# The last chunk's state product of a gated SSM and GELU mix as seven block products, with its block sums on VectorE

## The chip, the cores and the metric

The kernel runs on one core of a Trainium2 chip. The metric is the device time of one execution in microseconds. Before the change it is 211.94 us, the median of 3 runs (211.27 to 212.22). The engines are named as in the profile: PE (TensorE matmuls), PEld (its weight loads), DVE (VectorE), ACT (ScalarE), POOL (GpSimd) and SP (SyncE, which here only issues DMAs).

## The reference

For x of 2048 x 640 in bf16, a gate g mixes a state space layer a and a dense layer b:

```python
g = sigmoid((x * gate_w).sum(-1, keepdims=True))
h[t] = Lam_bar * h[t-1] + B_bar @ x[t]            # 640 complex states
a = 2.0 * (hseq @ Cmat.T).real + x * Dskip
b = gelu(x @ w1 + b1, approximate=True) @ w2 + b2 # 640 -> 1728 -> 640
out = g * a + (1 - g) * b
```

## The kernel before

Time is cut into 4 chunks of 512 rows (`NCH`, `CH`), each into 4 tiles of 128 rows (`TPC`). For each chunk c there are four stages.

- `ssm(c)` multiplies x by B (PE, line 607), copies the results to `bu` (ACT, line 610) and queues the scan for each of 5 groups of 128 states. One group's scan on DVE is `scan_ops`: two products, a sum, two scans (line 555), two products and the last difference into `hs[c]` (all products and sums come from the helper on line 533). Real and imaginary parts are the two halves of `hs[c]`, 1280 rows in all.
- `ff1(c)` is the first dense layer (PE, line 299) with GELU (ACT, line 308). The result `gel[c]` is laid out as two halves of time (i) by two halves of the hidden rows (k): four blocks a, b, g21, d.
- `fin_b(c)` is the second dense layer as seven block products in place of eight (2 x 2 blocks, in the manner of Strassen and Winograd): `both` does a product for the two tiles of a half on PE (line 702), 14 matmuls of 320 columns. Banks X, Y, Q and Z collect the products. `fork` copies a bank on ACT (line 714), `out_of` writes a bank scaled by 1 - g into `gb` on ACT (line 722), `part_7` writes -(1 - g) Q into `gq` on ACT (line 735), and POOL adds that to `gb` by an accumulating DMA (`plus`, line 650). The sums of left blocks, N3 and N2, and the sums g21 + d and b + N2, are made by a negation on ACT (line 655) and accumulating DMAs (`minus_c`, `minus_d`, and `plus(flat(b), flat(N2[:]))` inside `fin_b`). For chunk 0 `first_sums` does them on DVE (line 685). The sums of w2's blocks (TA, TB, TC) are made once, near the start.
- `fin_a(c)` is the state product, row tile by row tile: for each half of the 640 columns 10 matmuls (5 for the real, 5 for the imaginary part, line 775) add to a bank that `seed` has filled with x * Dskip (ACT, line 641; the product with Dskip is `skip`, DVE, line 635). DVE then writes `ot` = g * bank + `gb` (line 780), and SP stores it. The last tile is cut into 320, 192 and 128 columns, and ACT's queue stores the last piece. `ot` has three buffers.

The order of the work is written by hand. Each engine executes its instructions in the order of the calls. Only the scans are placed by a small model: `later` puts an operation on a list with a cost, `let_out(t)` emits what the model's DVE would have started by the model's time t, and `dve_now` first lets out what is due and then emits its own instruction. `Clock` holds the model's times. `fin_a(c)` begins with `let_out(0, c)`, which emits all that is left of chunk c's scans. SP's and POOL's queues take their DMAs in the order of the calls as well, and each waits in its place. `load_xn` on SP brings a tile of x back for the skip term; `seed(ti)` issues the load of tile ti + 5 into the buffer that it frees (five buffers).

The last part of the program is: `ssm(3)`, `ff1(3)`, `gates(3)`, `fin_b(2)`, `fin_a(2)`, `fin_b(3)`, `fin_a(3)`. So PE does chunk 3's states early, while DVE's scans for them run beside `ff1(3)`, `fin_b(2)`, `fin_a(2)` and a part of `fin_b(3)`.

Of the kernel before, what the change touches and what calls it, by code (L numbers as in the profile page):

```python
# [42 lines left out]
def kernel(  # L43
# [25 lines left out]
    ps = ctx.enter_context(tc.tile_pool(name="ps", bufs=8, space=bass.MemoryType.PSUM))  # L69
    hsp = ctx.enter_context(tc.tile_pool(name="hsp", bufs=2))  # L70
    gelp = ctx.enter_context(tc.tile_pool(name="gelp", bufs=2))
    xnp = ctx.enter_context(tc.tile_pool(name="xnp", bufs=5))
    work = ctx.enter_context(tc.tile_pool(name="work", bufs=2))
    fwork = ctx.enter_context(tc.tile_pool(name="fwork", bufs=4))

# [7 lines left out]
    n1c = F - cut2 + 1  # L83
    xA, xB = (const.tile([P, KD, CH], BF16, name=n) for n in ("xA", "xB"))
    xT = [xA, xB, xB, xA]
    w1a = [const.tile([P, cut1], BF16, name=f"w1a_{kd}") for kd in range(KD)]
    w1b = [const.tile([P, cut2 - cut1], BF16, name=f"w1b_{kd}") for kd in range(KD)]
    w1c_lo = const.tile([P, 3, n1c], BF16, name="w1c_lo")
    w1c_hi = const.tile([P, 2, n1c], BF16, name="w1c_hi")
    w1c = [w1c_lo[:, j, :] for j in range(3)] + [w1c_hi[:, j, :] for j in range(2)]  # L90
    w2_sb = const.tile([P, 2, KF, HD], BF16, name="w2_sb")
# [30 lines left out]
    def load_xn(ti):  # L122
        xn[ti] = xnp.tile([P, D], BF16, name="xn")
        nc.sync.dma_start(out=xn[ti][:], in_=x2d[ti * P:(ti + 1) * P, :])
# [2 lines left out]
        nc.sync.dma_start_transpose(out=xT[c][:], in_=x2d[c * CH:(c + 1) * CH, :])  # L127

    def load_w1a(queue, kd):
        queue.dma_start(out=w1a[kd][:], in_=B_w1[kd * P:(kd + 1) * P, 0:cut1])  # L130

    def rows(queue, dst, v):
        queue.dma_start(out=dst, in_=v.rearrange("(j p) -> j p", p=P))
# [25 lines left out]
    load_w1a(nc.sync, 4)  # L159
    load_w1a(nc.sync, 3)  # L160
    for kd in range(KD):
        nc.sync.dma_start(out=w1b[kd][:], in_=B_w1[kd * P:(kd + 1) * P, cut1:cut2])
    for t, k0, k1 in ((w1c_lo, 0, 3), (w1c_hi, 3, KD)):
        nc.sync.dma_start(out=t[:, :, 0:F - cut2], in_=B_w1[k0 * P:k1 * P, cut2:F].rearrange("(k p) f -> p k f", p=P))
    make_identity(nc, ident[:])
    HC = CH // 8
    tfi = work.tile([P, HC], I32, name="e")
    nc.gpsimd.iota(tfi[:], pattern=[[1, HC]], base=0, channel_multiplier=0)
    rows(nc.gpsimd, prmA[0:KS, :], A_log_dt)
    rows(nc.gpsimd, prmA[KS:2 * KS, :], A_Lambda_im)  # L170
# [39 lines left out]
    def load_skip():  # L210
        nc.sync.dma_start(out=Dbc[:], in_=A_Dskip.rearrange("(o d) -> o d", o=1).to_broadcast([P, D]))
        for a in range(TPC):
            load_x0(nc.sync, a, KA * P, D)
        load_xn(TPC)

    ctx.enter_context(tc.manual_schedule(engines={E.PE, E.DVE, E.Activation, E.SP, E.Pool}))

# [22 lines left out]
    def dve_now(ready, cost, fn):  # L240
        let_out(ready)
        fn()
        ck.dve = max(ck.dve, ready) + cost
# [282 lines left out]
    def scan_ops(c, ks, bu, ready):  # L526
        wide = lambda t: t[:, ks:ks + 1, :].to_broadcast([P, 2, CH])
        signed = c > 0
        sines = TSIN2[:, ks, :, :] if signed else wide(TSIN)
        s = {}  # L530

        def tt(o, a, b, op):
            nc.vector.tensor_tensor(out=o, in0=a, in1=b, op=op)  # L533

        def f1():
            s["mc"] = work.tile([P, 2, CH], BF16, name="wa", bufs=1)
            tt(s["mc"][:], wide(TCOS), bu[:], ALU.mult)

        def f2():
            s["ms"] = work.tile([P, 2, CH], BF16, name="wb", bufs=1)  # L540
            tt(s["ms"][:], sines, bu[:], ALU.mult)

        def f3():
            s["v"] = work.tile([P, 2, CH], BF16, name="v", bufs=1)
            if signed:
                return tt(s["v"][:], s["mc"][:], s["ms"][:, ::-1, :], ALU.add)
            tt(s["v"][:, 0, :], s["mc"][:, 0, :], s["ms"][:, 1, :], ALU.add)
            tt(s["v"][:, 1, :], s["mc"][:, 1, :], s["ms"][:, 0, :], ALU.subtract)

        def f4(ri):  # L550
            if ri == 0:
                settle(1)
                s["g"] = work.tile([P, 2, CH], BF16, name="g")
            init = 0.0 if c == 0 else carry[:, ri, ks:ks + 1]
            nc.vector.tensor_tensor_scan(s["g"][:, ri, :], r_c[:, ks:ks + 1].to_broadcast([P, CH]),  # L555
                                         s["v"][:, ri, :], init, ALU.mult, ALU.add)

        def f5():
            g = s["g"]

            def turn_carry():
                m = work.tile([P, 2], F32, name="e1")
                one = lambda out, i, sc, b: nc.scalar.activation(out=out, in_=g[:, i, CH - 1:CH], func=ACT.Identity,
                                                                 scale=sc[:, ks:ks + 1], bias=b)
                one(m[:, 0:1], 1, nsL, 0.0)
                one(m[:, 1:2], 0, sL, 0.0)
                one(carry[:, 0, ks:ks + 1], 0, cL, m[:, 0:1])
                one(carry[:, 1, ks:ks + 1], 1, cL, m[:, 1:2])
                ck.act += 0.6

            small.append((ck.dve + 2.0, turn_carry))

        def f6():
            s["no"] = work.tile([P, 2, CH], BF16, name="wa", bufs=1)
            tt(s["no"][:], wide(TCOS), s["g"][:], ALU.mult)

        def f7():
            s["ns"] = work.tile([P, 2, CH], BF16, name="wb", bufs=1)
            tt(s["ns"][:], sines, s["g"][:], ALU.mult)

        def f8():
            if signed:
                return tt(hs[c][:].rearrange("p (r k) t -> p r k t", r=2)[:, :, ks, :], s["no"][:], s["ns"][:, ::-1, :], ALU.subtract)
            tt(hs[c][:, ks, :], s["no"][:, 0, :], s["ns"][:, 1, :], ALU.subtract)
            tt(hs[c][:, KS + ks, :], s["ns"][:, 0, :], s["no"][:, 1, :], ALU.add)

        later(ready, 0.68, f1)
        later(0, 0.62, f2)
        later(0, 0.65 if signed else 0.7, f3)
        later(0, 1.27, lambda: f4(0))  # L590
        later(0, 1.21, lambda: f4(1))
        if c < NCH - 1:
            later(0, 0.0, f5)
        later(0, 0.69, f6)
        later(0, 0.62, f7)
        later(0, 0.64 if signed else 0.77, f8, c)

    def ssm(c, at={}):
        hs[c] = hsp.tile([P, 2 * KS, CH], BF16, name="hs")
        for ks in range(KS):  # L600
            if ks in at:
                at[ks]()
# [34 lines left out]
    def seed(ti):  # L637
        seeded[ti] = []
        for d0, d1 in cuts(ti):
            p = bank()  # L640
            nc.scalar.activation(out=p[:, 0:d1 - d0], in_=xn[ti][:, d0:d1], func=ACT.Identity)  # L641
            act(0.45)
            seeded[ti].append(p)
        if ti % TPC < TPC - 2:
            skip(ti + 2)
        if ti + 5 < NT:
            load_xn(ti + 5)

    def plus(dst, src):
        nc.gpsimd.dma_start(out=dst, in_=src, accum_op=ALU.add)  # L650
# [110 lines left out]
    def fin_a(c, at={}):  # L761
        let_out(0, c)
        for a in range(TPC):
            ti = c * TPC + a
            lo = a * P
            ot = fwork.tile([P, D], BF16, name="ot", bufs=3)
            if a < TPC - 2:
                seed(ti + 2)
            if a in at:
# [1 line left out]
            for i, (d0, d1) in enumerate(cuts(ti)):  # L771
                p = seeded[ti][i]
                for j in range(2 * KS):
                    CT = CT_re if j < KS else CT_im
                    nc.tensor.matmul(p[:, 0:d1 - d0], lhsT=hs[c][:, j, lo:lo + P], rhs=CT[:, j % KS, d0:d1],  # L775
                                     start=False, stop=(j == 2 * KS - 1), skip_group_check=True)
                    pe(d1 - d0)

# [10 lines left out]
            if ti < NT - 1:  # L789
                nc.sync.dma_start(out=out2d[ti * P:(ti + 1) * P, :], in_=ot[:])  # L790

    def skips(c):
        skip(c * TPC)
        skip(c * TPC + 1)

    def seeds(c, more=lambda: None):
        return {1: lambda: seed(c * TPC), 2: lambda: (seed(c * TPC + 1), more())}
# [23 lines left out]
    fin_a(1, sums(2))  # L821
    ssm(3)
    gel_tile(3)
    ff1(3)
    gates(3)
    skips(2)
    fin_b(2, seeds(2, lambda: minus_c(3)))
    minus_d(3)
    fin_a(2)
    skips(3)  # L830
    fin_b(3, seeds(3))
    let_out(1e9)
    fin_a(3)


# [28 lines left out]
```

## Time and profile before

| | |
|---|---|
| median of the runs | 211.94 us |
| the profiled execution: time | 212.2 us |
| its span, from the first to the last instruction | 210.4 us |
| PE busy | 204.3 us |
| DVE busy | 180.0 us |
| ACT busy | 142.7 us |
| `fin_b(3)` on PE | 182.75 to 196.3 us |
| `fin_a(3)` on PE | 196.4 to 207.5 us |
| last DVE instruction ends | 207.9 us |

The span is what the profile shows instruction by instruction; the time also holds what lies around it. A row of the timeline gives the start, the duration, the engine, the line, the operation, the tile written and the tiles read, the count of merged instructions, and, in brackets, the idle time of the engine before it and what ended it. A row of a group gives the count, the total and mean duration, and the idle time before its instructions.

### The profile page before, as it was taken

What the parts mean: (1) busy time and instruction counts of PE and PEld (TensorE: products, weight loads), DVE (VectorE), ACT (ScalarE), POOL (GpSimd) and SP (SyncE); (2) the same over time, 40 slices, a digit from 0 to 9 for tenths busy, and PEclk for the clock granted to TensorE, in tenths of its full rate; (3) what the DMA queues carried; (4) which work ended last, traced back from release to release, by engine and by line L of the source; (5) the groups of instructions that cost most, each with busy time, mean ns of one, the idle gap of its engine ahead of it and who ended that gap; (6) DMA issues with size and microseconds to landing.
All of it is one profiled execution on the core that took longest, in us unless ns stands there. A gap on an engine that the chain in (4) does not pass through costs nothing.

```text
span 210.4 us, 3617 instructions
## 1 busy us (share of the span) xinstructions
PE 204.3 (97%) x1326; PEld 122.0 (58%) x1326; DVE 180.0 (86%) x295; ACT 142.7 (68%) x290; POOL 48.3 (23%) x79
## 2 busy tenths in 40 slices
PE   8999999989999998999999999999999999999994
PEld 5745444444477543576457777544447777767773
DVE  2579999999997899596999999999999999998132
ACT  3499979996768799990674896267586594047600
POOL 8345059314310500031001043200000145010400
PEclk9999999999999999999999999999999999999999
DMA  7999999999997250249842379910001629943721
GB/s 181 243 189 203 199 247 283 205 231 173 158 190 184 38 90 0 62 86 236 189 101 44 78 119 205 234 49 0 0 0 27 125 64 178 215 131 79 112 78 62
DMA packets 42582, 27.82 MB, mean 132 GB/s; under 512 B 26594, under 2 KB 40388, under 8 KB 42564
## 3 DMA queue, kind: packets, MB, share of 16 engines
q1 hardware_dynamic: 36628, 16.21, 32.4%
q0 software_dynamic: 5360, 10.89, 30.2%
q10 hardware_dynamic: 576, 0.49, 0.7%
q8 instruction: 10, 0.16, 0.3%
q14 instruction: 8, 0.07, 0.1%
HBM read 7.79 MB, written 2.62 MB: 49 GB/s over the span
## 4 chain that ended last, share of the span: by engine, by line
PE 45%; DVE 33%; ACT 12%; issue 5%; DMA 3%; SPq 1%; DVEq 0%
PE bank L607 15%; DVE g L555 11%; PE bank L702 10%; PE bank L775 10%; PE bank L299 8%; DVE wa L533 6%; DVE wb L533 6%; ACT gel L308 5%; DVE hs L533 3%; DVE v L533 3%; DMA xn<-in_A_x_dram 3%; DVE ot L780 3%; PE bank L323 1%; DVE xn L635 1%; ACT TB L655 1%
## 5 line engine op out<-in xcount | busy, mean ns | idle before, releaser
L775 PEld LDWEIGHTS <-hs 128*128 128x128 bf16 x330 | 31.6, 98 | 11.9
L555 DVE TENSOR_TENSOR_SCAN g<-r_c,carry,v 128x512 bf16<-128x512 f32 x30 | 37.2, 1271 | 0.8
L610 ACT ACTIVATE bu<-bank 128x512 bf16<-128x512 f32 x40 | 23.1, 594 | 19.0 <-PE bank L607 18.9
L308 ACT ACTIVATE gel<-bank,colB 128x512 bf16<-128x512 f32 (+1 forms) x52 | 32.9, 694 | 3.0 <-PE bank L299 2.8
L702 PEld LDWEIGHTS <-gel 128*128 128x128 bf16 x280 | 27.2, 98 | 11.0
L780 DVE SCALAR_TENSOR_TENSOR ot<-bank,gcol,gb 128x320 bf16<-128x320 f32 (+2 forms) x33 | 17.5, 531 | 11.8 <-PE bank L775 5.1
L775 PE MATMUL bank<-CT_im,hs 128*128 128x320 bf16 (+2 forms) x165 | 27.1, 295 | 0.0
L775 PE MATMUL bank<-CT_re,hs 128*128 128x320 bf16 (+2 forms) x165 | 27.1, 295 | 0.0
L702 PE MATMUL bank<-w_sb,gel 128*128 128x320 bf16 x168 | 24.1, 299 | 0.0
L299 PEld LDWEIGHTS <-w1a 128*128 128x128 bf16 x162 | 14.4, 101 | 11.9
L722 ACT ACTIVATE gb<-bank,gcol 128x320 f32<-128x320 f32 x32 | 16.1, 525 | 6.0 <-PE bank L702 6.0
L714 ACT ACTIVATE bank<-bank 128x320 f32<-128x320 f32 x16 | 6.8, 424 | 16.5 <-PE bank L702 16.5
L650 POOL DMA_DIRECT2D gel<-N x4 | 3.4, 856 | 60.8 <-PE bank L702 51.2
L607 PEld LDWEIGHTS <-BT_im 128*128 128x128 bf16 x100 | 9.8, 98 | 11.8
L607 PEld LDWEIGHTS <-BT_re 128*128 128x128 bf16 x100 | 9.6, 98 | 11.0
L650 POOL DMA_DIRECT2D gb<-gq x8 | 10.4, 1624 | 22.6 <-ACT gb L722 22.6
L533 DVE TENSOR_TENSOR v<-wa,wb 128x1024 bf16<-128x1024 bf16 (+1 forms) x25 | 14.2, 584 | 0.6
L299 PE MATMUL bank<-xA,w1a 128*128 128x128 bf16 (+2 forms) x102 | 14.6, 302 | 0.0
L533 DVE TENSOR_TENSOR wa<-TCOS,bu 128x1024 bf16<-128x1024 bf16 x20 | 13.7, 687 | 0.6
L533 DVE TENSOR_TENSOR wa<-TCOS,g 128x1024 bf16<-128x1024 bf16 x20 | 13.8, 688 | 0.4
L641 ACT ACTIVATE bank<-xn 128x320 f32<-128x320 bf16 (+2 forms) x33 | 12.7, 427 | 1.7 <-DVE xn L635 1.5
L533 DVE TENSOR_TENSOR wb<-TSIN,g 128x1024 bf16<-128x1024 bf16 x20 | 13.7, 683 | 0.0
(146 smaller groups left out, 354.7 us busy)
## 6 DMA issues: line engine op xcount, KB each, us to landing
gb<-gq POOLq DMA_DIRECT2D x8, 320.0 KB, 5.4
out_dram<-ot SPq DMA_DIRECT2D x15, 160.0 KB, 3.8
w_sb<-in_B_w_dram SPq DMA_DIRECT2D x4, 480.0 KB, 6.5
xn<-in_A_x_dram SPq DMA_DIRECT2D x12, 160.0 KB, 3.9
gel<-N POOLq DMA_DIRECT2D x4, 448.0 KB, 4.5
N<-gel POOLq DMA_DIRECT2D x3, 448.0 KB, 4.5
gel<-gel POOLq DMA_DIRECT2D x3, 448.0 KB, 6.4
N<-N POOLq DMA_DIRECT2D x3, 448.0 KB, 7.8
```

The costliest lines, as they stand in the source:

```text
L299: nc.tensor.matmul(p[:, t0:t1], lhsT=w, rhs=xT[c][:, kd, t0:t1], start=(kd == 0) if first is None else first, stop=(kd == last), skip_grou ...
L308: nc.scalar.activation(out=dst, in_=src, func=ACT.Gelu_apprx_tanh, bias=b1_c[p0:p1, kf:kf + 1])
L533: nc.vector.tensor_tensor(out=o, in0=a, in1=b, op=op)
L555: nc.vector.tensor_tensor_scan(s["g"][:, ri, :], r_c[:, ks:ks + 1].to_broadcast([P, CH]), s["v"][:, ri, :], init, ALU.mult, ALU.add)
L607: nc.tensor.matmul(p[:], lhsT=BT[ks >= KSA][:, kd, (ks % KSA if ks < KSA else ks - KSA) * P:][:, 0:P], rhs=xT[c][:, kd, :], start=(kd == 0 ...
L610: nc.scalar.activation(out=bu[:, ri, :], in_=p[:], func=ACT.Identity)
L641: nc.scalar.activation(out=p[:, 0:d1 - d0], in_=xn[ti][:, d0:d1], func=ACT.Identity)
L650: nc.gpsimd.dma_start(out=dst, in_=src, accum_op=ALU.add)
L702: nc.tensor.matmul(p[:, 0:HD], lhsT=lhs[:, s, j * P:(j + 1) * P], rhs=rhs[:, s, :], start=fresh and s == 0, stop=s == KH - 1, skip_group_c ...
L722: nc.scalar.activation(out=gbs[ti][:, h * HD:(h + 1) * HD], in_=quad[j][name][:, 0:HD], func=ACT.Identity, scale=gcol[:, 1, ti:ti + 1])
L775: nc.tensor.matmul(p[:, 0:d1 - d0], lhsT=hs[c][:, j, lo:lo + P], rhs=CT[:, j % KS, d0:d1], start=False, stop=(j == 2 * KS - 1), skip_group ...
L780: nc.vector.scalar_tensor_tensor(out=ot[:, d0:d1], in0=p[:, 0:d1 - d0], scalar=gcol[:, 0, ti:ti + 1], in1=gbs[ti][:, d0:d1], op0=ALU.mult, ...
```

## The change

Only the two products of chunk 3 are done in a new way, and what they need is prepared along the way.

- `last_a(3)` does the state product as seven block products: two halves of time by real and imaginary part on the left (`hs` is now stored as half of time, part, group, row, so that a block is contiguous), and real and imaginary part by two halves of the 640 columns on the right. A product has 5 matmuls of 320 columns for each of two tiles, 70 in all (75 with the last one cut in two).
- The block sums of C (U5, U6, U7, U4) are made by two negations on ACT inside `ff1(3)`, two plain copies on SP's queue and four accumulating DMAs on POOL's queue. They lie in tiles that are free by then (B's, x's and w1's; w1's tiles are joined for that).
- The block sums of `hs` (M7, g21, M6, M3) are four instructions of DVE (`h_sums`), after the last scan.
- `last_b(3)` does the same seven dense products as `fin_b(3)` in a new order. Bank additions that ACT and POOL did are now done on DVE: Z = X - q and Q = X - q for two tiles each (`less`), b + N2 (`evened`), and the eight evictions into `gb` (`done`). Their second operand is no bank's seed but `GS`, g * x * Dskip, which ACT writes from x (`gated`); so chunk 3 has no `seed`, and its state product starts from empty banks. `last_b` and `last_a` share `last_product`. All of chunk 3's remaining scans are let out after product 7, before the first sum.
- The four `skip`s of chunk 3 come together, ahead of `last_b`.
- `ot` has four buffers in place of three, `xn` four in place of five; `seed(ti)` loads tile ti + 4, and the early load of tile 4 is gone.

```diff
-    xnp = ctx.enter_context(tc.tile_pool(name="xnp", bufs=5))
+    xnp = ctx.enter_context(tc.tile_pool(name="xnp", bufs=4))
...
-        hs[c] = hsp.tile([P, 2 * KS, CH], BF16, name="hs")
+        hs[c] = hsp.tile([P, 2, 2, KS, HT], BF16, name="hs")
...
-        if ti + 5 < NT:
-            load_xn(ti + 5)
+        if ti + TPC < NT:
+            load_xn(ti + TPC)
...
-            ot = fwork.tile([P, D], BF16, name="ot", bufs=3)
+            ot = fwork.tile([P, D], BF16, name="ot", bufs=4)
...
+    def h_sums(c):
+        (a, b), (g21, d) = ([hs[c][:, i, r] for r in range(2)] for i in range(2))
+        steps = []
+        for out, x, y, op in ((M7, a, g21, ALU.subtract), (g21, g21, d, ALU.add), (M6, a, g21, ALU.subtract), (M3, b, M6, ALU.add)):
+            steps.append(lambda fn=add(out, x, y, op): dve_now(0, 0.8, fn))
+        return steps, (a, M7, M6, b, g21, M3, d), (C11, U7, U6, C21, U5, C22, U4)
...
+    def last_product(lhs, rhs, done, evened=None, at={}, tail=False):
...
+        def less(out, j):
+            t = out[j] = out[j] or bank()
+            dve_now(ck.pe + 0.2, 0.52, lambda: nc.vector.tensor_tensor(out=t[:, 0:HD], in0=X[j][:, 0:HD], in1=q[j][:], op=ALU.subtract))
...
+        for j in range(H):
+            product(X, 1, j, True)
+            Y[j] = bank()
+            nc.scalar.activation(out=Y[j][:, 0:HD], in_=X[j][:, 0:HD], func=ACT.Identity)
+            act(0.45)
+        for j in range(H):
+            product(Q, 7, j, True)
+            q[j] = fwork.tile([P, HD], F32, name="gq", bufs=2)
+            nc.scalar.activation(out=q[j][:], in_=Q[j][:, 0:HD], func=ACT.Identity)
+            act(0.53)
+        hook(0)
+        for j in range(H):
+            product(X, 6, j)
+            less(Z, j)
+        hook(1)
+        for j in range(H):
+            product(Y, 2, j)
+        if evened:
+            dve_now(ck.pe + 0.2, 1.1, evened)
+        for j in range(H):
+            product(X, 5, j)
+            less(Q, j)
+        for j in range(H):
+            done(Y[j], j, 0, 0)
+        for j in range(H):
+            done(Q[j], j, 1, 1)
+        hook(2)
+        for j in range(H):
+            product(X, 3, j)
+            done(X[j], j, 0, 1)
+        for j in range(H):
+            cols = ((0, 192), (192, HD)) if tail and j == H - 1 else ((0, HD),)
+            product(Z, 4, j, False, cols)
+            done(Z[j], j, 1, 0, *cols[-1])
...
+        last_product(lhs, rhs, done, add(lhs[3], lhs[3], lhs[2], ALU.add),
+                     {0: lambda: (gated(c), let_out(1e9), sums[0]()), 1: lambda: (sums[1](), sums[2]()), 2: sums[3]})
...
-    ff1(3)
+    nc.sync.dma_start(out=U4, in_=C21)
+    ff1(3, 0, {1: lambda: c_minus(0), 4: lambda: (c_minus(1), plus(U5, C12))})
+    nc.sync.dma_start(out=U7, in_=C12)
     gates(3)
     skips(2)
-    fin_b(2, seeds(2, lambda: minus_c(3)))
+    fin_b(2, seeds(2, lambda: (plus(U7, U6), minus_c(3))))
     minus_d(3)
-    fin_a(2)
-    skips(3)
-    fin_b(3, seeds(3))
-    let_out(1e9)
-    fin_a(3)
+    fin_a(2, {1: lambda: plus(U6, U5), 3: lambda: plus(U4, U6)})
+    for a in range(TPC):
+        skip(NT - TPC + a)
+    steps, lhs, rhs = h_sums(3)
+    last_b(3, steps)
+    last_a(3, lhs, rhs)
```

## The prediction

> **What bounds the kernel now.** The profiled execution has a span of 210.4 us and a time of 212.2 us, so 1.8 us lie around the span. The median of the three runs is 211.94 us, 0.26 less. I sum against 212.2 and take 0.2 off at the end.
>
> I read the page first, and its busy shares alone mislead:
>
> ```profile
> PE 204.3 (97%) x1326; PEld 122.0 (58%) x1326; DVE 180.0 (86%) x295; ACT 142.7 (68%) x290; POOL 48.3 (23%) x79
> DVE  2579999999997899596999999999999999998132
> PE 45%; DVE 33%; ACT 12%; issue 5%; DMA 3%; SPq 1%; DVEq 0%
> ```
>
> PE looks like the bound, and ten matmuls less look like time won. But the slices show DVE full from about 100 us to 190 us, and the third line (the chain that ended last) has 33% on DVE. In order of time that chain runs on DVE from 119.85 to 186.8 us and on PE from there on. So the last chunk has two limits: PE, which never waits after 87 us, and DVE, which is late with chunk 3's states while PE already works on chunk 3's feed-forward product. The timeline of DVE and PE at the end shows how late:
>
> ```profile
> 187.75 0.88 DVE L635 TENSOR_TENSOR xn<-xn,Dbc 128x640 bf16<-128x640 bf16 x2
> 188.55 2.45 DVE L555 TENSOR_TENSOR_SCAN g<-r_c,carry,v 128x512 bf16<-128x512 f32 x2
> ...
> 190.74 2.06 PE L702 MATMUL bank<-TA,gel 128*128 128x320 bf16 x14
> ...
> 192.62 0.69 DVE L533 TENSOR_TENSOR hs<-wa,wb 128x1024 bf16<-128x1024 bf16 x1
> ...
> 196.44 0.84 PE L775 MATMUL bank<-CT_re,hs 128*128 128x320 bf16 x5
> ...
> 198.06 0.55 DVE L780 SCALAR_TENSOR_TENSOR ot<-bank,gcol,gb 128x320 bf16<-128x320 f32 x1 [4.34 <-ACT bank L641]
> ```
>
> The last part of hs comes at 192.62 + 0.69 = 193.3 us; its first reader starts at 196.4, so 3 us are spare. DVE is idle for 4.34 us before 198.06 and for some 5 us between the later evictions: about 9.4 us of idle DVE in the tail. The change spends that.
>
> A third view, DVE's waits over the whole span, has a line that the change touches elsewhere (the timeline puts it at 98.2 to 100.3 us, in chunk 0's state product):
>
> ```profile
> DVE ot L780 <- DMA out_dram<-ot: 2.2, 1, 2.2
> ```
>
> **The change, part by part.**
>
> *PE.* The 80 full-width matmuls of chunk 3's state product (in 90 pieces) become 70. Five take 0.68 us from start to start (196.44 to 197.12 in the same timeline), so 10 less save 1.36 us. The feed-forward product keeps its 98 matmuls in another order.
>
> *`ot` with four buffers.* The fourth output tile of chunk 0 no longer waits for the first one's store. Its products were ready at about 97 us, so the 2.17 us are won, and DVE is the bound behind it. I checked whatever could take them back. Chunk 2's bu are written by 109.9 us and read from 117.7 on. In fin_a(1), an eviction moved 2.17 us earlier still starts 0.3 to 1.5 us after its matmuls end (4 tiles x 1.36 us per half from 122.9 us); in fin_a(2) by 3 us or more. gb<-gq of chunk 2 lands, as I estimate, by about 180 and 182 us (N3, g21, gq, gq in order, 448 and 320 KB, at the 178 GB/s of the stretch from 172.5 us on) and would be wanted at 181.0 and 184.0. I take the whole 2.17 us as kept; the other bound is 0.
>
> *DVE's order behind it.* All four skips now stand ahead of the last scans (one more than before: 0.40 us). So: 187.75 + 4 x 0.40, scans 2.50, two products 0.61 + 0.71, hs 0.73: the next instruction would start at 193.9, less 2.17 gives 191.73 us. From there the order is fixed: one state sum, Z = X - q twice, two state sums, the sum for b, Q = X - q twice, four evictions, the fourth sum, four evictions; then four differences and nine evictions for the state product. Prices by these rows (mean ns of one):
>
> ```profile
> L685 DVE TENSOR_TENSOR N<-gel 128x1792 bf16<-128x1792 bf16 x2 | 2.2, 1088 | 0.0
> L533 DVE TENSOR_TENSOR v<-wa,wb 128x1024 bf16<-128x1024 bf16 x15 | 10.4, 690 | 0.5
> L780 DVE SCALAR_TENSOR_TENSOR ot<-bank,gcol,gb 128x320 bf16<-128x320 f32 x31 | 16.7, 541 | 11.4 <-PE bank L775 4.8 <-ACT bank L641 4.3 <-DMA out_dram<-ot 2.2
> ```
>
> A state sum has 1280 columns: between 0.69 and 1.09, by the slope 0.82 us. The b sum is the 1792 row. A difference that writes a bank is in no row: from 0.49 (128x320 f32 in SBUF, line 456) to 0.55; I take 0.54, the row that reads a bank. An instruction that waits for nothing starts 0.09 before its predecessor's end (evictions 0.45 apart).
>
> *The new wait.* Product 5 adds into X, and X must first be read by Z = X - q, which stands on DVE behind the last hs and a state sum. PE is ready for it at 190.7 us (182.75 us and four products of 2.0 us). The difference runs from 192.46 to 193.0. So PE stands from 190.7 to 193.1: **2.4 us**. Behind the difference on DVE: two sums to 195.0, b to 196.04, Q = X - q to 196.50. Product 3 adds into X too and reads b: PE, done with product 5 at 195.0, stands until 196.6: **1.6 us** more. Products 3 and 4 end at 200.4 us. In before that point was 196.3: +4.1 us. (fork, q copies and the scaling of x stay on ACT and end by 191; ACT loses 16 evictions and seeds, some 8 us, which nobody waits for. If ACT were late, the evictions from 197 on would wait, with 6 us of cover.)
>
> *The state product.* 200.4 + 70 x 0.136 = 209.9, and 0.2 for product 3, which waits for Q = X - q once more: 210.1 us on PE (before: 207.4). DVE then has eight evictions' worth of work behind product 5, in a row: Q = X - q ends at 208.0, then four evictions that product 2 and 5 had long made possible but that were queued behind it, then X, X, Z and the two pieces of the last: 207.92 + 7 x 0.45 + 0.33 + 0.35 = **211.75 us** (before: 207.88). So the tail is DVE's, 1.1 us behind what PE alone would give (210.1 + 0.27 + 0.35). That eats most of the 1.36 us.
>
> *Stores.* Three 160 KB stores now go out within 1.4 us instead of 2.7 us apart; the page's median to landing is 3.8 us, the lowest seen 1.8. Before, the span ended 2.5 us after DVE. I add 0.4 (bounds 0 and 1.3).
>
> *At no cost.* Two negations of 1600 columns on ACT in ff1(3), about 1.5 us each by the 1792-column row (1.69): ACT is busy for 13.9 of 18.5 us there; without that cover PE would wait for a bank as it did twice at 83 to 87 us (1.0 and 0.3 us), and the 2.4 us of standing would swallow it. The copies into U4, U7 on SP's queue and four accumulating DMAs on POOL's, 400 KB each: one POOL issue now stands ahead of N3's. At those 178 GB/s each takes 2.3 us; U7 falls into the quiet stretch 167.5 to 171.5 us, U6 and U4 come behind N2 and land by about 195 us, wanted at 203 and later. Late by more than 1 us, U7 would push gb<-gq into DVE's evictions (below). x with four buffers: tile 15's load now stands behind chunk 2's first store on SP, about 178 us, wanted at 187. The new hs layout writes rows of 256 instead of 512: 0.69 as now, or, if it costs as two halves do (0.42 each, line 533 of chunk 0), 0.15 more for each of the ten on the DVE chain, 1.5 us. I take nothing. The joined w1 tiles load in the same order.
>
> *Sum*: 212.2 + (211.75 - 207.88) + 0.4 = 216.5; less 0.2: **216.3 us**.
>
> [...] The clock first, as the trace has it (stretches; the clock stands behind the busy times):
>
> ```profile
> 209.00:210.20 1.20, 0.00 (x0) 0.00 (x0) 0.00 (x0) 0.00 (x0) 0.00 (x0) 1.00 0.01 1
> 210.30:210.40 0.10, 0.00 (x0) 0.00 (x0) 0.00 (x0) 0.00 (x0) 0.00 (x0) 0.55 0.00 0
> ```
>
> The granted clock falls 2.8 us after the last matmul's end, while 1.04 us of standing at 83 us left it alone. A gap of 2.4 us lies between. A slow start is seen too: the first nine matmuls take 2.72 us for 3072 columns, 2.1 times the later pace. So a fall would cost up to about 1 us (product 5 takes 3.8 instead of 1.9 us, most of it inside the 1.6 us that PE would stand anyway). I take no fall.
>
> [...]
>
> [...]
>
> **Rivals.**
> 1. *The 2.17 us are lost again* (gb<-gq lands late behind U7, or an eviction meets its matmuls). DVE is ready at 193.9, PE stands 4.5 us: 218.5 us. With a clock fall or the dearer hs, 219.5 and above. For it: margins of about 1 us at gb<-gq. Against: they are margins.
> 2. *Not slower: DVE is ahead of product 5.* If chunk 3's states were ready some 4 us earlier than I have them (first sum by 187.7 us), both stands vanish, the state product starts at 196.5, and the end is DVE's at 207.85: 212.4 us, no change; with a shorter eviction tail 211.3. Up to 4 us each us of earlier states gives one back. For it: PE is 97% busy and its work shrinks. Against: DVE has no idle time from 101 to 193 us, so nothing but the 2.17 us can come earlier.
> 3. *The prices are too high*: product 3 waits only for b, differences at 0.49: 214.6 us.
>
> **How the numbers follow.** My forecast with rival 3 as its lower edge has 0.62, rival 1 has 0.28, rival 2 has 0.10. The range, 214.4 to 219.4, leaves out rival 2 and the dearest ends of rival 1. About 0.5% (1.06 us) is what a measurement of this kernel can tell from no change. Slower by more: 0.90; within it: 0.07; faster by more: 0.03, since even rival 2 needs a shorter tail as well.
>
> **What would show it.** Right: no wait for a store in DVE's list at 98 us; PE waiting for DVE twice, once over 2 us before product 5 and once about 1.6 us before product 3; the last DVE instruction over 1 us behind the last matmul. Wrong: chunk 3's last hs before 189 us, or after 193; PE without a wait in the feed-forward product; a granted clock under 1.00 before 205 us; a PE wait for U4, U6 or U7.

## The result and the profile after

The change makes the kernel slower: 218.49 us, the median of 6 runs (218.00 to 219.69), against 212.08 us of the kernel before in the same session (6 runs). The ratio is 1.0314, with a 95% interval of 1.0284 to 1.0344. The prediction said 216.3 us, slower, in a range of 214.4 to 219.4: the direction is right, the time is inside the range, and 2.2 us are missing in the sum.

The profiled execution of after is the slowest of the six: 219.69 us, span 217.9 us. The spans of the other five are 216.2 to 217.1 us. So 0.8 to 1.7 us of what its trace shows may be this execution's own. (Here and below, a ratio leaves out an execution that is over 1.5% above the fastest of its kernel.)

From the page of after (busy times, DVE's slices, the granted clock's slices):

```profile
PE 206.0 (95%) x1311; PEld 122.4 (56%) x1311; DVE 191.0 (88%) x316; ACT 141.6 (65%) x281; POOL 48.6 (22%) x80
DVE  1589999999969899699999999999999999898463
PEclk9999999999999999999999999999999999976999
```

DVE has 11 us more work than before, as the diff says. PE has 15 instructions less and yet 1.7 us more busy time. The third line tells why: two slices near the end are at 7 and 6 tenths of the clock, where before shows a 9 in every slice (1.00 from the start to 210.2 us).

The timeline of DVE and PE at the end of after:

```profile
184.52 0.55 DVE L782 SCALAR_TENSOR_TENSOR ot<-bank,gcol,gb 128x320 bf16<-128x320 f32 x1 [0.30 <-issue]
...
188.33 0.49 DVE L638 TENSOR_TENSOR xn<-xn,Dbc 128x640 bf16<-128x640 bf16 x1 [0.99 <-DMA xn<-in_A_x_dram]
188.74 2.45 DVE L556 TENSOR_TENSOR_SCAN g<-r_c,carry,v 128x512 bf16<-128x512 f32 x2
...
192.55 0.69 DVE L534 TENSOR_TENSOR hs<-wa,wb 128x1024 bf16<-128x1024 bf16 x1
193.28 0.82 DVE L806 TENSOR_TENSOR BT_re<-hs 128x1280 bf16<-128x1280 bf16 x1
194.02 0.89 DVE L846 TENSOR_TENSOR bank<-bank,gq 128x320 f32<-128x320 f32 x2
...
194.57 3.89 PE L837 MATMUL bank<-TA,gel 128*128 128x320 bf16 x14 [3.50 <-DVE bank L846]
198.25 3.11 PE L837 MATMUL bank<-w_sb,gel 128*128 128x320 bf16 x14
...
203.09 1.52 PE L837 MATMUL bank<-CT_re,hs 128*128 128x320 bf16 x10
...
210.50 3.62 DVE L912 SCALAR_TENSOR_TENSOR ot<-bank,gcol,gb 128x320 bf16<-128x320 f32 x8
...
214.17 0.44 PE L837 MATMUL bank<-xB,hs 128*128 128x128 bf16 x5 [1.59 <-DVE ot L912]
214.64 0.35 DVE L912 SCALAR_TENSOR_TENSOR ot<-bank,gcol,gb 128x128 bf16<-128x128 f32 x1 [0.53 <-PE bank L837]
```

Read it from the top. DVE stands 0.30 us before an eviction of tile 11. The profile names no releaser, but the second accumulating DMA `gb<-gq`, which this eviction needs, was issued at 173.4 us and landed 11.0 us later, at 184.4. Then DVE waits 0.99 us for a tile of x, so the last part of `hs` comes at 192.55 us, where before had it at 192.62: a lead is gone. Product 5 (`bank<-TA,gel`) waits 3.50 us for Z = X - q, which stands on DVE behind the first state sum. Products 5 and 3 then take 3.7 and 2.9 us from start to start instead of 1.9. The state product starts at 203.09 (before: 196.4). In the tail, DVE evicts eight pieces in a row, and the last five matmuls wait 1.59 us for one of them.

SP's queue shows where the tile of x was late. Column two is the time that the issues took, as the profile has it:

```profile
177.96 0.35 SPq L792 DMA_DIRECT2D out_dram<-ot  x1
178.37 1.37 SPq L126 DMA_DIRECT2D xn<-in_A_x_dram  x1
```

The load is issued at 178.4 and DVE goes on at 188.3, 9.9 us later; the page's median for this load is 5.2 us. Beside it run the accumulating DMA into U6 (`BT_im<-BT_re`, 12.2 us from issue to landing) and three stores.

Last, the granted clock in stretches of 0.1 us (behind the busy times):

```profile
193.50:193.60 0.10, 0.00 (x0) 0.00 (x0) 0.10 (x1) 0.00 (x0) 0.00 (x0) 0.69 0.01 0
...
200.20:200.30 0.10, 0.10 (x2) 0.07 (x1) 0.10 (x2) 0.00 (x0) 0.00 (x0) 0.50 0.00 0
200.30:200.40 0.10, 0.10 (x3) 0.02 (x1) 0.10 (x2) 0.00 (x0) 0.00 (x0) 0.68 0.00 0
```

The clock is 1.00 in the stretch ahead of the first row, 0.50 from 193.6 to 200.3 us, and 1.00 again from 200.4 to 217.4 us. Between these levels, 0.69 puts the fall at 193.54 us, 2.5 us after the last matmul ended (189.00 + 2.07), and 0.68 the return at 200.36: the clock stood at 0.50 for 6.8 us.

### The profile page after: what moved, and what is told of

The parts are those of the page before. It is cut to its first block, busy times and chain, and to the rows that moved or that the text cites. A ratio compares the mean times of both kernels' runs of the same rounds, so it can differ in the third digit from the quotient of the medians.

```text
span 217.9 us, 3612 instructions
## 1 busy us (share of the span) xinstructions
PE 206.0 (95%) x1311; PEld 122.4 (56%) x1311; DVE 191.0 (88%) x316; ACT 141.6 (65%) x281; POOL 48.6 (22%) x80
## 4 chain that ended last, share of the span: by engine, by line
PE 32%; DVE 30%; SPq 12%; DMA 10%; ACT 10%; issue 5%; DVEq 0%
PE bank L610 10%; DVE g L556 10%; PE bank L705 7%; PE bank L837 7%; PE bank L777 6%; ACT gel L309 5%; DMA xn<-in_A_x_dram 5%; DVE wa L534 5%; DVE wb L534 4%; DMA w_sb<-in_B_w_dram 3%; DVE hs L534 3%; DVE v L534 3%; SPq L184 2%; SPq L185 2%; DVE ot L912 2%
## 5 line engine op out<-in xcount | busy, mean ns | idle before, releaser
L777 PEld LDWEIGHTS <-hs 128*128 128x128 bf16 x240 | 23.4, 98 | 9.1
L705 PEld LDWEIGHTS <-gel 128*128 128x128 bf16 x210 | 20.5, 98 | 8.2
L300 PEld LDWEIGHTS <-w1a_sb 128*128 128x128 bf16 x162 | 14.6, 102 | 11.9
L777 PE MATMUL bank<-CT_re,hs 128*128 128x320 bf16 x120 | 20.2, 300 | 0.0
L777 PE MATMUL bank<-CT_im,hs 128*128 128x320 bf16 x120 | 20.2, 299 | 0.0
L300 PE MATMUL bank<-xA,w1a_sb 128*128 128x128 bf16 (+2 forms) x102 | 14.7, 303 | 0.0
L534 DVE TENSOR_TENSOR wb<-TSIN,bu 128x1024 bf16<-128x1024 bf16 x20 | 13.7, 685 | 0.0
L300 PE MATMUL bank<-xB,w1a_sb 128*128 128x512 bf16 x60 | 13.3, 380 | 0.0
L782 DVE SCALAR_TENSOR_TENSOR ot<-bank,gcol,gb 128x320 bf16<-128x320 f32 x24 | 12.8, 542 | 0.4 <-issue 0.3
L300 PEld LDWEIGHTS <-w1b_sb 128*128 128x128 bf16 x80 | 7.8, 97 | 9.5
```

The costliest lines, as they stand in the source:

```text
L300: nc.tensor.matmul(p[:, t0:t1], lhsT=w, rhs=xT[c][:, kd, t0:t1], start=(kd == 0) if first is None else first, stop=(kd == last), skip_grou ...
L705: nc.tensor.matmul(p[:, 0:HD], lhsT=lhs[:, s, j * P:(j + 1) * P], rhs=rhs[:, s, :], start=fresh and s == 0, stop=s == KH - 1, skip_group_c ...
L777: nc.tensor.matmul(p[:, 0:d1 - d0], lhsT=hs[c][:, a // H, j // KS, j % KS, (a % H) * P:][:, 0:P], rhs=CT[:, j % KS, d0:d1], start=False, s ...
L782: nc.vector.scalar_tensor_tensor(out=ot[:, d0:d1], in0=p[:, 0:d1 - d0], scalar=gcol[:, 0, ti:ti + 1], in1=gbs[ti][:, d0:d1], op0=ALU.mult, ...
```

## The experiments

Theory after this reading: the time is set by one chain on DVE (last x tile, scans, `hs`, sums, differences, evictions), of which PE's stands are the image; three things made it later than predicted: the late load of x, the clock, and the wait of the cut last piece. Rivals: the clock alone, DVE's amount of work whatever its order, and, for each half of the change, that the half costs the same by itself.

The first four runs share 18 runs of before (median 212.19 us).

**Tile 15's load ahead of tile 8's store** (`early_x`).

```diff
+            if held:          # in the next tile, behind its seed()
+                held.pop()()
...
-            if ti < NT - 1:
-                nc.sync.dma_start(out=out2d[ti * P:(ti + 1) * P, :], in_=ot[:])
+            if c == 2 and a == 0:
+                held.append(store)
+            elif ti < NT - 1:
+                store()
```

> The changed kernel, but the store of tile 8 is issued on SP's queue behind the load of x's tile 15, not ahead of it. In the changed kernel's trace that load is issued at 178.4 us, lands 9.9 us later, and VectorE waits for it at 187.3 to 188.3 us. Theory (VectorE's lateness with chunk 3's states sets the end, one for one): the load is issued about 2.4 us earlier and lands before 187 us, the wait of 1.0 us goes, the last hs comes 1.0 us or more earlier, PE's first stand shrinks from 3.5 to about 2.3 us, and the time falls by 1.0 us, to 217.5; by about 2 us, to 216.4, if the clock no longer falls in the shorter stand. Rival (the accumulating DMAs for U6 and U4 fill the DMA engines, the place in the queue does not matter): the load still lands at 188 us, 218.5 us.

Measured: 217.62 us (216.85 to 218.35), ratio 1.0245 [1.0218, 1.0271]. From its timeline:

```profile
184.10 0.55 DVE L785 SCALAR_TENSOR_TENSOR ot<-bank,gcol,gb 128x320 bf16<-128x320 f32 x1 [0.67 <-issue]
...
185.63 1.69 DVE L638 TENSOR_TENSOR xn<-xn,Dbc 128x640 bf16<-128x640 bf16 x4
...
191.05 0.69 DVE L534 TENSOR_TENSOR hs<-wa,wb 128x1024 bf16<-128x1024 bf16 x1
...
193.07 3.58 PE L843 MATMUL bank<-TA,gel 128*128 128x320 bf16 x14 [2.35 <-DVE bank L852]
```

All four skips run without a wait, and `hs` and product 5 come 1.5 us earlier. The stand is now 2.35 us, the prediction's 2.4. Not all of the 1.5 us is the load's: this execution was 0.86 us ahead already when PE began `last_b(3)` (182.09 against 182.95). The rest, 0.64 us, is the 0.99 us of the load's wait less what a longer wait takes back, 0.67 us in place of 0.30 before tile 11's eviction, where `gb<-gq` landed at 184.1. The median gains 0.9 us, about the 1.0 that was expected if the clock still fell, and in the profiled execution it did (0.50 from 193 to 196 us; product 5 takes 3.58 us).

**PE kept at work during the stand** (`warm`). 36 extra matmuls of 192 columns go to columns of a bank that nobody reads.

```diff
+            for n in range(36):
+                nc.tensor.matmul(Q[n % H][:, HD:512], lhsT=A[2][:, 0, 0:P], rhs=B[2][:, 0, 0:512 - HD], start=True, stop=True, ...)
             dve_now(ck.pe + 0.2, 1.1, evened)
```

> The changed kernel, with 36 matmuls of 192 columns ahead of product 5 of the dense layer, into columns 320 to 511 of Q's banks, which nothing reads. They fill 3.0 of the 3.5 us that PE stands there. Theory (the halved clock behind the stand costs PE some 1.2 us of its own): granted clock 1.00 throughout, product 5 takes 2.1 us again instead of 3.9, time 217.3 us (217.0 to 217.6). Rival (PE's slow products hide behind VectorE's sums): clock 1.00, but the time stays at 218.5 us, within 0.3.

Measured: 218.22 us (217.34 to 218.52), 1.027 [1.0243, 1.0297], clock 0.996 to 1.000. PE's rows:

```profile
194.36 2.06 PE L837 MATMUL bank<-TA,gel 128*128 128x320 bf16 x14 [1.09 <-DVE bank L846]
197.75 2.06 PE L837 MATMUL bank<-w_sb,gel 128*128 128x320 bf16 x14 [1.33 <-DVE bank L846]
```

Product 5 is fast again (2.06 us, 3.89 in after), and product 3 then waits 1.33 us for the second Q = X - q. What the clock gives back, DVE's two sums and b + N2 take. The expected 217.3 was missed: with the state sums where they are, the fallen clock costs the median only some 0.3 us. (The profiled execution of after, with 6.8 us at 0.50, took 219.69 us, that of `warm` 218.12.)

**The last piece uncut** (`uncut`).

```diff
-        last_product(lhs, rhs, done, tail=True)
+        last_product(lhs, rhs, done)
```

> The changed kernel with the last product of the last tile in one piece of 320 columns. In the changed kernel the last five matmuls (128 columns) stand 1.6 us for VectorE's eviction of the first 192 columns of the same bank. Theory (that wait is on the path, but VectorE's row of evictions is nearly as late): the last eviction starts at once behind the one before, ends 0.3 to 0.6 us earlier, time 218.0 us. Rival (the cut pays for itself by the smaller last store): 218.5 us or more.

Measured: 217.50 us (216.98 to 218.82), 1.0251 [1.0222, 1.0279]: 1.0 us less, twice what was expected. The tail's rows:

```profile
208.99 3.75 DVE L912 SCALAR_TENSOR_TENSOR ot<-bank,gcol,gb 128x320 bf16<-128x320 f32 x8
```

The last of the eight ends at 212.74, and nothing follows. The cut was meant to let the first 192 columns be evicted while PE does the last 128, but both lie in one bank; the last matmuls wait for DVE's read of the first part (1.59 us in after), which is queued behind seven others. In before the pieces had banks of their own.

**Buffers alone** (`ot4`): before, with four `ot` and four `xn` buffers.

```diff
-    xnp = ctx.enter_context(tc.tile_pool(name="xnp", bufs=5))
+    xnp = ctx.enter_context(tc.tile_pool(name="xnp", bufs=4))
-            ot = fwork.tile([P, D], BF16, name="ot", bufs=3)
+            ot = fwork.tile([P, D], BF16, name="ot", bufs=4)
```

> The kernel before with only the buffers changed: four for ot, four for x (loads for tile ti + 4). Theory (VectorE gets 2 us ahead, but in the kernel before its states are not what the end waits for): VectorE's wait for a store at 98 us goes, the last hs comes at about 191.3 instead of 193.3 us, and the time stays within 0.5 us of 212.1. Rival (VectorE's chain from 100 to 187 us sets the end): 210 us.

Measured: 212.12 us, 0.9999 [0.9975, 1.0023]. The last `hs` starts at 190.81 instead of 192.62. So the fourth buffer does win its time for DVE, and before cannot use it, since PE sets its end.

The next four share 23 runs of before (median 212.35 us).

**The dense half alone** (`dense_only`): `last_b`, then the old `fin_a(3)` from empty banks; no block sums of C or `hs`.

```diff
-    last_b(3, steps)
-    last_a(3, lhs, rhs)
+    last_b(3, [lambda: None] * 4)
+    fin_a(3)
```

> The changed kernel with the new dense product of chunk 3 (its bank additions, b + N2 and evictions on VectorE, GS as second operand), but the state product as before, tile by tile, from empty banks; no sums of C or hs. Theory (the stands of PE behind VectorE are the cost, and each VectorE instruction ahead of them is paid): without the state sum ahead of Z = X - q and without late loads PE stands some 1.6 us before product 5 and hardly before product 3; the state product, 80 matmuls, starts at about 198.1 instead of 196.3 us: 213.9 us (213.3 to 214.6). Rival A (the seven-block state product is what costs): 212.2 us. Rival B (the new dense product costs all of it): 218 us.

Measured: 213.45 us, 1.0053 [1.0033, 1.0072], as expected. Tile 15's load, still behind tile 8's store, lands 8.2 us after its issue, and DVE doesn't wait for it. PE stands 1.37 us before product 5 and not before product 3, and the mean clock is 0.998 to 1.000.

**The state half alone** (`state_only`): the old dense product, with POOL's additions of gq and the skip term added to `gb` by DVE, the state sums beside it, then `last_a`.

```diff
-    last_b(3, steps)
+    fin_b(3, {1: lambda: gated(3), 2: lambda: (let_out(1e9), [s() for s in steps]),
+              4: lambda: scaled((2, 3)), 5: lambda: scaled((0, 1))})   # gb += GS on DVE
     last_a(3, lhs, rhs)
```

> The other half: the dense product of chunk 3 in the old order with ScalarE's evictions and the accumulating DMA for b; VectorE adds -(1 - g) Q and the skip term GS to gb. The state product as in the changed kernel, seven block products, with its sums and its cut last product. Theory: PE has no stand in the dense product, the state product starts at 196.3 us, VectorE's four sums and six additions end by 201 us, just in time; the tail (eight evictions in a row, and the last 128 columns behind them) ends 0.8 us later than before: 213.2 us (212.6 to 213.8). Rival A (the state product's own additions make PE wait): 216 us or more. Rival (ten matmuls less): 211 us.

Measured: 214.32 us, 1.0087 [1.0054, 1.0121]. Missed by 0.5 us and more. PE waits 1.63 us for b + N2, which in this kernel is a DMA again.

**The state half with what was known by then** (`state_best`): `state_only` with the early load, the uncut last piece, and the first evictions of the state product early.

```diff
             product(Y, 2, j)
+            if not evened:
+                done(Y[j], j, 0, 0)
...
-            done(Y[j], j, 0, 0)      # behind product 5
+            if evened:
+                done(Y[j], j, 0, 0)
```

> As state_only, and: tile 15 of x loaded ahead of tile 8's store; in the state product the two evictions of Y directly behind product 2, ahead of Q = X - q; the last product uncut. Theory: PE ends at about 206.1 us, 1.3 us earlier than in the kernel before, and VectorE's last eviction ends 0.9 us behind it, at 207.0 (207.9 in the kernel before); the stores take 0.2 to 0.4 back: 211.6 us (211.2 to 212.2). Rival (the tail stays VectorE's or the stores'): 212.6 us or more.

Measured: 214.07 us, 1.0077 [1.0048, 1.0107]: no gain, and a clear miss. The rows of POOL's queue and PE say why:

```profile
177.59 1.21 POOL L653 DMA_DIRECT2D BT_im<-BT_re  x1
190.55 0.86 POOL L653 DMA_DIRECT2D xB<-BT_im  x1 [11.74 <-DMA BT_im<-BT_re]
191.09 1.20 POOL L653 DMA_DIRECT2D gel<-N  x1
...
197.06 2.08 PE L705 MATMUL bank<-w_sb,gel 128*128 128x320 bf16 x14 [2.16 <-DMA gel<-N]
```

`gel<-N` is b + N2. It stands on POOL behind `xB<-BT_im` (U4 += U6), which waits 11.7 us for U6 to land, so it is issued at 191.1 us; PE would need it at 194.9. Moreover the twelve executions fall into two groups of six: 212.6 to 213.7 us at a mean clock of 1.000, and 214.5 to 215.3 at 0.992.

**The whole change with four mends** (`all_four`): early load, 22 idle matmuls, uncut last piece, first evictions early.

> The changed kernel with four mends at once: tile 15 of x loaded earlier (0.9 us measured alone), the last product uncut (1.0 us measured alone), 22 idle matmuls in the stand before product 5 (36 of them gave 0.3 us alone), and in the state product Y's evictions ahead of Q = X - q (estimate 0.8 us). Theory (these are the tail and the extras; the stands remain): 215.5 us (215.0 to 216.2), with PE standing for VectorE some 2 and 1.6 us as before. Rival (the mends remove the cost): 213 us or less.

Measured: 215.71 us, 1.0149 [1.012, 1.0177], as expected. PE still waits 0.55 us (behind the idle matmuls, which fill 2.0 us of that stand) and 1.33 us for DVE.

The next three share 15 runs of before (median 212.29 us).

**The state sums behind what PE waits for** (`sums_late`).

```diff
-                     {0: lambda: (gated(c), let_out(1e9), sums[0]()), 1: lambda: (sums[1](), sums[2]()), 2: sums[3]})
+                     {0: lambda: (gated(c), let_out(1e9)), 2: sums[0]})
+        for s in sums[1:]:
+            s()
```

> The change with the order of DVE alone altered: no sum of the state blocks stands ahead of Z = X - q, the sum for b or Q = X - q; the first stands behind product 5's evictions, the other three behind the last eviction of the feed-forward product. Theory (PE's two stands come from DVE's order, and 1.6 to 2.4 us of sums stand ahead of what PE waits for): product 5 starts 0.8 us earlier, no wait before product 3, the state product starts about 200.5 instead of 203.1, 216.0 us (215.5 to 216.8). Rival (the same work on DVE before the state product's end, in whatever order, gives the same end): 218.2 to 218.8.

Measured: 217.67 us, 1.0231 [1.0184, 1.0277], outside the expected range and short of the rival's, in two groups: 215.8 us at a clock of 0.996 to 0.997 (two executions, the profiled one among them), and 217.6 to 218.9 at 0.987 to 0.990 (four). In the profiled one:

```profile
193.35 2.06 PE L837 MATMUL bank<-TA,gel 128*128 128x320 bf16 x14 [3.06 <-DVE bank L846]
...
199.05 1.52 PE L837 MATMUL bank<-CT_re,hs 128*128 128x320 bf16 x10
```

The order works as the theory has it (no wait before product 3, state product 4 us earlier than in after), but the median shows it only in part. The suspicion: without sums to hide behind, a fallen clock is paid in full.

**The same with PE kept at work** (`late_warm`), run afterwards on that suspicion (11 runs of before, 212.40 us). The edit is that of the first run with extra matmuls.

> The change with the state sums late, as in the run before, plus 36 matmuls of 192 columns whose result nobody reads, put where PE stands for Z = X - q, so that the array is never idle for more than about 1 us there. The run before had two groups of executions: 215.8 us at a mean granted clock of 0.996 to 0.997, and 217.6 to 218.9 us at 0.987 to 0.990. Theory (the groups differ by the clock that falls in the 3 us stand, and with DVE's sums out of the way nothing hides that any more): all executions at 0.995 or above, 215.8 us (215.3 to 216.4). Rival (the groups differ by something else, and the clock only goes with it): the median stays at 217 or more, or two groups remain.

Measured: 216.17 us (215.70 to 216.94), 1.0177 [1.0147, 1.0207], clock 0.993 to 1.000. There is one group, around 216, and the profiled execution has no wait of PE but the one for the cut last piece. So the slower group goes away when the stand does, as it must if it was the clock's (six executions). Two of them lie at 0.993 and 0.994, below the expected 0.995. The mean clock also counts the fall behind the last matmul (the 0.996 of `sums_late`'s profiled execution is all of that kind, from 212.26 us on). A stretch like that of `early_x`, 3.4 us at 0.50, takes 0.008 off a mean over 214 us, so 0.993 and 0.994 leave no room for one of that length; a shorter one is not ruled out.

**The change with its order mended** (`five`): sums late, early load, uncut last piece, first evictions early; no idle matmuls.

> The change with tile 8's store behind tile 15's load, the last piece uncut, the first evictions of the state product early, and the state sums late as in the kernel beside it; no idle matmuls. Theory (the single gains add up where they lie on one chain: the load's 1 us brings the last hs forward, the sums' order 1.6 to 2.4 us): about 1 to 1.5 us of wait before product 5, none before product 3, clock 1.00, state product starts about 199.5 us, 213.8 us (213.2 to 214.8): half of the change's loss mended, still slower than before. Rival (the sums, put late, are what the state product then waits for): PE waits for DVE inside the state product by over 1 us in sum, 215 or more.

Measured: 213.57 us (213.10 to 214.19), 1.0062 [1.0041, 1.0082], as expected. PE waits 1.49 us before product 5, the state product starts at 198.15, the clock is 0.998 to 1.000. Of the 6.4 us that the change cost, 4.9 were the order of the work and the cut piece.

**The state half with POOL's order mended** (`state_mend`): `state_best` with one line moved.

```diff
-    fin_a(2, {1: lambda: plus(U6, U5), 3: lambda: plus(U4, U6)})
+    fin_a(2, {1: lambda: plus(U6, U5)})
...
-    fin_b(3, {1: lambda: gated(3), ...
+    fin_b(3, {1: lambda: (plus(U4, U6), gated(3)), ...      # behind b + N2
```

> The combination for the state product alone, with one accumulating DMA moved: U4 += U6 is issued behind chunk 3's b += N2 on POOL instead of ahead of it, so that b's sum no longer stands behind a transfer that waits for U6. Theory (the 2.2 us that PE stood for b were POOL's order, and nothing but the order; a stand that is gone also leaves the clock at 1.00): no wait of PE for b, granted clock 1.00 in every execution, state product starts about 196.5 us in the span, last DVE instruction about 206.5, 211.2 us (210.8 to 211.8), faster than both kernels. Rival 1 (the queue of 400 KB transfers is late by itself, whoever stands first): PE still waits for b by over 1 us, 213 to 214. Rival 2 (DVE's row of evictions and the last stores set the end, whatever PE gains): no wait for b, but 212.3 or more.

Measured: 210.99 us, 0.9931 [0.9906, 0.9955], faster than both kernels. Six of its seven executions lie at 210.5 to 211.2 us and a clock of 0.998 to 1.000; the seventh, at 0.991, took 214.1. The timeline:

```profile
187.54 0.86 POOL L653 DMA_DIRECT2D gel<-N  x1 [9.51 <-issue]
189.76 0.86 POOL L653 DMA_DIRECT2D xB<-BT_im  x1 [1.36 <-DMA BT_im<-BT_re]
...
193.95 2.06 PE L705 MATMUL bank<-w_sb,gel 128*128 128x320 bf16 x14
195.85 1.52 PE L849 MATMUL bank<-CT_re,hs 128*128 128x320 bf16 x10
...
203.25 2.93 DVE L927 SCALAR_TENSOR_TENSOR ot<-bank,gcol,gb 128x320 bf16<-128x320 f32 x6
204.07 1.52 PE L849 MATMUL bank<-xB,hs 128*128 128x320 bf16 x10
```

PE no longer waits for b, and the state product starts at 195.85. It ends at 205.59: 9.74 us, where before took 11.05 (196.44 to 207.49). DVE ends at 206.18 (before: 207.88). So seven block products for the state do win about 1.3 us on PE, where their sums cost PE no wait. The four `ot` buffers, which this kernel also has, are no rival: alone they changed nothing (`ot4`). The seventh execution misses the expected clock of 1.00, and no trace shows why.

## Why the prediction was right, and where it fell short

- *What bounds, and the mechanism.* Right: the last chunk is a race of PE and DVE, and the change puts DVE work in front of a product that adds into the same bank. PE waits for DVE before product 5, as predicted, but for 3.50 us in place of 2.4. The second wait, before product 3, isn't in after: at a clock of 0.50 product 5 ends at 198.46 us, when DVE's first Q = X - q (197.90) is done. `sums_late` and `five` confirm the mechanism from the other side: less DVE work in front of PE's next product, less time. `state_mend` shows the same for a sum on POOL's queue.
- *PE's 1.36 us.* Right: a pair of tiles takes 1.36 us (10 matmuls), and in `state_mend` the state product takes PE 1.3 us less than before.
- *`ot`'s fourth buffer: 2.17 us, kept.* This step failed. They are won (no store wait at 98 us; chunk 2's evictions start at 176.95 instead of 178.98) and then largely lost, as rival 1 had it. What the rival named, gb<-gq, did land late: at 184.4 us, where the prediction had "about 182" and wanted it at 184.0. It cost DVE 0.30 us in after and 0.67 in `early_x`. The larger part is tile 15's load, "wanted at 187" and costed at nothing. It landed 9.9 us after its issue, at 188.3, and held DVE for 0.99 us. DVE's first state sum started at 193.28 instead of 191.73. `early_x` shows the load's worth: 0.9 us of the median. That rival 1's 218.5 us is the measured time is luck: its stand was 4.5 us and without a fall of the clock.
- *The new wait.* With DVE on time the 2.4 us are met almost exactly (2.35 in `early_x`), in part by luck: there PE began `last_b(3)` 0.66 us earlier than the 182.75 that the sum took, and lost 0.69 us before product 6 to a DMA (`N<-N`) that the sum had left out. The 1.6 us before product 3 measure 1.33 in `warm`, where the clock holds at a mean of 0.999 (behind a stand that the idle matmuls had mostly filled). The prices under them hold too: state sum 0.82, difference 0.49 to 0.50 (taken 0.54), b sum 1.09, `hs` 0.69 in the new layout.
- *"I take no fall."* Wrong as a fact, nearly right as a price. The clock fell to 0.50 even in the 2.35 us stand of `early_x`, and product 5 took 3.58 us in place of 2.06 there, 3.89 in after. In after most of that lies beside DVE's sums (`warm`: 0.3 us in the median), as the prediction's bound of 1 us allowed. (The bound came from a slow start in which, 0 to 4 us of before, the trace has the clock at 1.00; it was an estimate.) Two executions of `early_x` have a mean clock of 0.993, which leaves no room for a stretch as long as the profiled one's 3.4 us, and they took 217.1 and 217.7 us, no less than the other three. Once the chain on DVE is shortened, the executions at a lower clock take 1.8 us (`state_best`'s groups) or 2.2 us (`sums_late`'s) longer.
- *The tail.* "7 x 0.45 + 0.33 + 0.35" missed a wait: the last five matmuls stand 1.59 us for an eviction from the same bank. `uncut` gains 1.0 us. The 1.1 us by which the tail was to lie behind PE is 1.0 by the prediction's own figures. The stores are as taken: the span ends 2.9 us behind DVE (2.5 + 0.4).
- *The sum.* Late load 0.9, cut piece 1.0, clock 0.3: 2.2 us, the difference between 216.3 and 218.5. The three were measured one at a time and against executions of another session, so that they add up so well is partly luck: by the ratios, each to before in its own session, they are worth 1.5, 1.3 and 0.9 us, 3.7 in all, each uncertain by almost 1 us.
- *The signs.* Of the signs of being right, the wait for a store is gone, and PE stands over 2 us before product 5. The second stand isn't there, and the last DVE instruction ends only 0.4 us behind the last matmul, because the cut piece made that matmul wait for DVE. Two signs of being wrong came: the clock fell before 205 us, and the last `hs` was complete at 193.24, after 193.
- *Halves.* The dense half alone costs 1.1 us, the state half 2.0 us as first built and -1.3 us with the early load, the uncut tail and POOL's order mended. So the state half's block products did not have to be slower; for the dense half no run found an order that is faster than before.

How long the clock stayed down differs from kernel to kernel: 6.8 us in after and, by the same reading, 3.4 us in `early_x`:

```profile
192.70:192.80 0.10, 0.00 (x0) 0.00 (x0) 0.10 (x1) 0.00 (x0) 0.00 (x0) 0.86 1.40 256
...
196.10:196.20 0.10, 0.10 (x2) 0.00 (x1) 0.10 (x1) 0.00 (x0) 0.00 (x0) 0.57 0.00 0
```

(0.86 puts the fall at 192.77, 0.57 the return at 196.19.) In `early_x` the fall came 2.05 us after the last matmul ended (190.72). In `uncut` it came only when PE had been back at work for 1.0 us (from 193.91 on, behind a stand of 3.54 us):

```profile
194.90:195.00 0.10, 0.10 (x2) 0.06 (x1) 0.08 (x1) 0.00 (x0) 0.00 (x0) 0.61 0.00 0
```

And the 3.06 us stand of `sums_late` (190.29 to 193.35) left the clock (third column from the end) at 1.00:

```profile
190.00:191.00 1.00, 0.29 (x3) 0.09 (x1) 0.96 (x2) 0.00 (x0) 0.00 (x0) 1.00 0.67 125
191.00:192.00 1.00, 0.00 (x0) 0.00 (x0) 1.00 (x2) 0.00 (x0) 0.00 (x0) 1.00 1.09 202
192.00:193.00 1.00, 0.00 (x0) 0.00 (x0) 0.97 (x3) 0.00 (x0) 0.00 (x0) 1.00 0.47 83
193.00:194.00 1.00, 0.65 (x5) 0.48 (x5) 1.00 (x3) 0.00 (x0) 0.00 (x0) 1.00 0.00 0
```

So in these traces the length of a stand does not tell by itself whether the clock falls: 2.35 us (`early_x`) had a fall, 3.06 us had none. What does decide was not shown. That a fall is also what parts the executions of one kernel into two groups is argued from their mean clocks, not shown: no execution of the slower groups (`state_best`, `sums_late`) was profiled.

Open: what makes tile 15's load slow. U6 is not most of it: `dense_only` and `ot4` have none of the four transfers for C's sums, and there the load takes 8.2 and 8.5 us. The accumulation into U6 takes 12.2 us to land, where those into U7 and U4, of the same 400 KB, take 4.7 and 4.0. In after the DMA engines are busy throughout this time (a share of 0.96 or more in every stretch of 2 us from 173 to 189 us), so both may simply have waited their turn; no run shows behind what.

## What to carry to other kernels

Saving matmuls pays only where the sums that pay for them lie outside the chain that PE waits on: write down, for each instruction that PE will wait for, what is queued ahead of it on its engine or DMA queue, and move everything else behind it. The same algorithm gave 218.5, 213.6 and, in one half alone, 211.0 us by order and an uncut last piece. A load or a DMA sum costed at nothing "because it is wanted later" needs a margin of more than a median landing time where other transfers start beside it (here 9.9 us against a median of 5.2).

## What the runs showed of the hardware that was not expected

- The granted clock fell 2.05 us (`early_x`) and 2.5 us (after) after the last matmul ended, and in `uncut` 1.0 us after PE was back at work. It stood at 0.50 for 3.4 us in `early_x` and `uncut` (192.77 to 196.19, 194.92 to 198.34) and for 6.8 us in after (193.54 to 200.36).
- A 3.06 us stand (`sums_late`, profiled execution) left the clock at 1.00, while 2.35 us in another kernel (`early_x`) did not. What parts them was not shown.
- A 160 KB load took 9.9 us beside an accumulating DMA of 400 KB and stores, against a median of 5.2 us, and 8.2 and 8.5 us without that accumulating DMA.
- The 3.4 us at 0.50 of `early_x` are 1.7 us of PE's work at full clock, an estimate from these two figures. A lower clock went with 0.3 us more of the medians (after against `warm`) and with 1.8 us between `state_best`'s groups; that the difference comes from what ran beside it is argued, not shown.
